# Contexts of two more units kept on the chip, and a new order of copies in the head, in a fused attention and two-layer kernel

## The chip, the cores and the metric

One core of one Trainium2 chip runs one launch of the program. The time is the device time of that launch in microseconds; a kernel's figure is the median of its runs.

## What is computed

The input is attention (4 batches, 8 heads, head size 64): 512 local tokens see 32 global tokens and a window of 32 to either side; the 32 global tokens see all 544. Then come two layers on the 2176 contexts of 512 columns:

```python
k_all = np.concatenate([k_g, k_l], axis=2)
v_all = np.concatenate([v_g, v_l], axis=2)
out_g = np.matmul(sm(scale * np.matmul(q_g, k_all.transpose(0, 1, 3, 2))), v_all)
s_ll = np.where(np.abs(pos[:, None] - pos[None, :]) <= window, s_ll, -1e9)
a_l = sm(np.concatenate([s_lg, s_ll], axis=-1))
out_l = np.matmul(a_l, np.concatenate([v_g, v_l], axis=2))
...
h = np.maximum(np.maximum(x @ w1, x @ w2), x @ w3)      # d_ff 768
x = h @ w_out
h = x @ w_in                                            # d_ff 2048
g = np.maximum(h, 0.0) + np.log1p(np.exp(-np.abs(h)))
out = g @ w_out
```

`sm` is the softmax with 1e-9 added to its sum. The weights lie in memory as 64-bit words and are turned into 32-bit floats on the chip.

## The kernel before

**Products.** TensorE multiplies a rounded format (fp32r). So each operand is split in two, a high part (a rounding copy, `xh`, `hh`, `w[:,0]`) and what is left (a subtraction, `xl`, `hl`, `w[:,1]`), and each product is three matmuls: high by high, high by low, low by high. In the first layer's up part a product `pu` has 12 matmuls (L516 to L518), in its down part `pd` has 18 (L562 to L564).

**Units.** The contexts are cut into 8 units of 256 columns (odd ones 288: 32 global columns are added). A unit's contexts come from four attention groups, `pr` 0 to 3, so there are 32 groups; group k belongs to unit k // 4. A unit takes 18 up products (three weights for each of six blocks f), the maximum of each three (`m`, L527 and L530), the split of the maximum (`split_h`, L545 to L548) and the down products.

**Attention as a stream.** `att_stream` is one generator; its step k issues, for different groups, the scores of group k (`s1`, `ps`, L142, one PSUM buffer, read by the masks L148 on VectorE), the products of group k-3 with the values (`s3`, `po`, L238 and L242) and the transposes of the probabilities of group k-2 (`s2`, `pw` and `pg`, L211 and L212). Behind them come, on ScalarE, the exps of group k (`s1e`, L155), the copy of `po` (`s3h`), the copies of the transposes (`s2e`, `pgt` L223, `pwt` L225, for odd k on VectorE, L227). POOL normalises group k-1 (L164, L165). The global tokens' scores are `psg` (`s1g`, L177 and L183, copied by L180 or L186), their softmax is `gsoft` (L195 to L201, in three pieces), its transposes `pb` and `pa` (`g2`, L272 and L275), its product with the values `pog` (`g3`, L294). Steps 0 to 11 (`KS = 12`) are the **head**; in steps 8 and 10 (and each other step in which `gq` is set) a global softmax is transposed.

**PSUM.** `ptile`, `up` and `down` draw from one pool of five banks in turn; a new tile waits until the last reader of its bank's former tile is done.

**Contexts of a unit.** Units 0 and 1 are split straight from PSUM: `xh` by ScalarE (L252), `xl` by VectorE (L263), global columns by L101 and L102. The others are copied to SBUF (`xo`, L255, or L305), written to memory (`xd`, L256, L307), and read back into `xr` when the unit before goes down (`load_x`, L110), then split (L113, L114). The pair `xh`, `xl` has two buffers.

**The order of the work.** Every engine runs its instructions in the order in which they are written here. All transfers are issued on one queue, SP's, in program order. Between the steps of the stream a loop puts up products of units 0 and 1 and pieces of the decode of weights (three or four operations on VectorE, L472 to L484, copies on ScalarE L452 and L458, the low part on POOL L453): this is how the 24 tiles of the first layer's weights come to be ready one by one. `pend` holds products whose copy or maximum is not yet issued; `rest` issues one, `flush` all. In unit 0's second down (`by_row`) the maxima of unit 1 are split, six at once. Then `AS = 4` more pieces of the stream follow, and unit 1's down products. `HLP = 3` sends the low part of the first three maxima of unit 0 to POOL.

Of the kernel before, what the change touches and what calls it, by code (L numbers as in the profile page):

```python
# [21 lines left out]
def body(ctx, tc, kq, vw, vb, qg, w1, w2, w3, w_out, w2_in, w2_out, out):  # L22
# [7 lines left out]
    HHA = 2  # L30
    HLP = 3
    XLP = 0
# [57 lines left out]
    st = {}  # L90
    xs = {}
    gs = {}
    xd = [dram.tile([128, 4, 288], F32, name=f"xd{i}") for i in range(8)]
# [5 lines left out]
    def split_x(u, ks, ns, p):  # L99
        xh, xl = xs[u] if u in xs else new_x(u)  # L100
        nc.scalar.activation(xh[:, ks, ns], p, AF.Copy)  # L101
        nc.vector.tensor_tensor(xl[:, ks, ns], p, xh[:, ks, ns].bitcast(F32), op=ALU.subtract)  # L102

    def load_x(u):
        n = 256 + 32 * (u % 2)
        xh, xl = new_x(u)
        xr = []
        for k in range(4):
            xr.append(hp.tile([128, 288], F32, tag="m", name="xr")[:, 0:n])
            nc.sync.dma_start(out=xr[k], in_=xd[u][:, k, 0:n])  # L110
        yield
        for k in range(4):
            nc.scalar.activation(xh[:, k, 0:n], xr[k], AF.Copy)  # L113
            (nc.gpsimd if XLP > u else nc.vector).tensor_tensor(xl[:, k, 0:n], xr[k], xh[:, k, 0:n].bitcast(F32), op=ALU.subtract)  # L114
            yield
# [51 lines left out]

    def s1g(k):
        b, hf, pr = groups[k]
        s, e = pr // 2, pr % 2  # L170
        g = st[k]
        ps = ptile([128, 288], "psg")
        ks = [st[k - 1]["kT"], g["kT"]]
# [56 lines left out]
    def s3(k):  # L230
# [13 lines left out]
        g["po"] = po  # L244

    def s3h(k):
        b, hf, pr = groups[k]
        po = st[k]["po"].rearrange("p u n -> p (u n)")
        if 2 * b + hf < 2:
            if hf not in xs:  # L250
                new_x(hf)
            nc.scalar.activation(xs[hf][0][:, pr:pr + 1, 0:256], po.unsqueeze(1), AF.Copy)  # L252
            return
        xo = at.tile([128, 256], F32, tag="xo", name="xo")
        nc.scalar.activation(xo, po, AF.Copy)  # L255
        nc.sync.dma_start(out=xd[2 * b + hf][:, pr, 0:256], in_=xo)  # L256

    def s3l(k):
        b, hf, pr = groups[k]
        po = st.pop(k)["po"].rearrange("p u n -> p (u n)")  # L260
        if 2 * b + hf < 2:
            xh, xl = xs[hf]
            nc.vector.tensor_tensor(xl[:, pr:pr + 1, 0:256], po.unsqueeze(1), xh[:, pr:pr + 1, 0:256].bitcast(F32), op=ALU.subtract)  # L263
# [20 lines left out]

    def g3(b, s):
        c = gs[b, s]
        gt, v0, v1 = c["gt"], c["v0"]["v"], c["v1"]["v"]
        vs = [(v0, 0, 128), (v0, 2, 128), (v1, 0, 128), (v1, 2, 64), (v1, 3, 96)]
        po = ptile([128, 2, 32], "pog")
        for e in range(2):  # L290
            for j, (v, u, n) in enumerate(vs):
                for i in range(2):
                    h = 2 * e + i
                    nc.tensor.matmul(po[64 * i:64 * i + 64, e, :], lhsT=v[0:n, u, 64 * h:64 * h + 64], rhs=gt[0:n, j, 32 * h:32 * h + 32],  # L294
                                     start=(j == 0), stop=(j == 4), skip_group_check=True)
        c["po"] = po

    def g3e(b, s):
        po = gs.pop((b, s))["po"]
        if b == 0:  # L300
            split_x(1, slice(2 * s, 2 * s + 2), slice(256, 288), po)
            return
# [5 lines left out]
    def att_stream():  # L308
# [18 lines left out]
        for k in range(n + 4):  # L327
            gq = None
            j = k - 3
            if 0 <= j < n and groups[j][1] == 1 and groups[j][2] % 2 == 1:  # L330
                gq = groups[j][0], groups[j][2] // 2
            if k < KS:
                s1(k, 0)
                s1(k, 1)
# [4 lines left out]
                if q2 is not None:  # L339
                    s2(q2)  # L340
                    p2 += 1
                for c in late:
                    g3(*c)
                s1e(k, 0)
                s1e(k, 1)
                if q3 is not None:
                    s3h(q3)
                if k:
                    s1f(k - 1)
                next(soft, None)  # L350
                if q2 is not None:
                    s2e(q2)
                if gq:
                    g2(*gq)
                elif gpend:
                    soft = gsoft()
# [6 lines left out]
                if k % 2 == 1:  # L363
                    s1g(k)
                for c in late:
# [184 lines left out]
    def down(u, c, by_row=False):  # L550
# [3 lines left out]
        for f0, f1 in [(f, f + 1) for f in range(6)] if by_row else ((0, 5), (5, 6)):  # L554
            for j in range(2):
                p = ps[j]
                cs = slice(128 * (c + j), 128 * (c + j) + 128)
                for f in range(f0, f1):
# [5 lines left out]
                    nc.tensor.matmul(p, lhsT=w[:, 1, cs], rhs=hh, start=False, stop=(f == 5))  # L564
        if by_row:
            for f in range(6):
                split_h(u + 1, f)
        for j in range(2):
# [235 lines left out]
    with tc.manual_schedule():  # L804
# [5 lines left out]
        AD = 3  # L810
        AS = 4
        D2 = 2.0
# [51 lines left out]
        def slot(u):  # L864
            f, i = divmod(pos[u], 3)
            up(u, f, i)
            pos[u] += 1

        def ready(u):
# [61 lines left out]
        for u in range(6):  # L931
# [11 lines left out]
            for v, f, i in pairs_of(u):  # L943
# [4 lines left out]
                if u == 5 and i == 2:  # L948
                    if f == 0:
                        ensure(6)  # L950
                        x6 = load_x(6)
                    next(x6, None)
            loads_x = [] if u == 0 else [7] if u == 5 else [u + 1]
            for v in loads_x:
                ensure(v)
            ldx = itertools.chain.from_iterable(load_x(v) for v in loads_x)
            if loads_x:
                next(ldx)
            for c in range(4):
# [9 lines left out]
            for _ in ldx:  # L969
                pass  # L970
            if u == 0:
                for _ in range(AS):
                    step()
# [437 lines left out]
```

## Time and profile before

| | |
|---|---|
| median of 3 runs | 780.06 us (778.52 to 780.24) |
| the profiled execution | 780.84 us |
| its span | 779.1 us |
| busy TensorE, VectorE, ScalarE, POOL | 750.6, 571.7, 373.4, 250.8 us |
| share of the span | 96%, 73%, 48%, 32% |
| mean granted clock of TensorE | 0.998 |
| memory traffic | 145.62 MB, 187 GB/s |

The profile is of one execution. Its times count from the start of its span. In an instruction's row the bracket gives the idle time of its engine before it and what ended it. A tile's name stands for all its buffers; `pu`, `pd`, `ps`, `pw`, `pg`, `po`, `psg`, `pog`, `pa`, `pb` lie in PSUM.

### The profile page before, as it was taken

The numbers are of one execution on the slowest core, as the hardware profiler recorded it, in microseconds if no ns is written. First come the engines' busy times: TensorE is split into PE (matmuls) and PEld (weight loads), VectorE is DVE, ScalarE is ACT, GpSimd is POOL, SyncE is SP. The second block draws the span as 40 slices with busy tenths as digits, with TensorE's granted clock in tenths as the row PEclk, the third lists the DMA queues.
The fourth block names the chain that finished last, engine by engine and source line by source line (L and its number), as shares of the span: only waits on it lengthen the run. The fifth ranks groups of instructions, "written<-read, shape, count | busy, mean of one in ns | idle before, by whom it ended". The sixth has DMA issues, their size and how long they took to land.

```text
span 779.1 us, 18128 instructions
## 1 busy us (share of the span) xinstructions
PE 750.6 (96%) x6984; PEld 722.0 (93%) x6984; DVE 571.7 (73%) x1438; ACT 373.4 (48%) x955; POOL 250.8 (32%) x240
## 2 busy tenths in 40 slices
PE   5779999999999999999999999999999999999998
PEld 3669998898999999999999999999999999999998
DVE  5978985677786686693991465544686889999996
ACT  5865445654554652233432455533554444444443
POOL 4544441112211210161960488943872000000000
PEclk9999999999999999999999999999999999999999
DMA  8938225777767746578010455445539923444432
GB/s 332 363 128 312 105 84 184 261 283 248 257 213 250 251 170 203 197 267 295 12 42 28 151 179 200 138 159 185 175 132 370 378 93 109 136 136 135 137 95 82
DMA packets 80742, 145.62 MB, mean 187 GB/s; under 512 B 10128, under 2 KB 45840, under 8 KB 80656
## 3 DMA queue, kind: packets, MB, share of 16 engines
q1 hardware_dynamic: 80656, 144.47, 53.9%
q8 instruction: 55, 0.90, 0.5%
q14 instruction: 31, 0.25, 0.1%
HBM read 98.63 MB, written 45.81 MB: 185 GB/s over the span
## 4 chain that ended last, share of the span: by engine, by line
PE 77%; DVE 8%; DMA 4%; ACT 4%; issue 3%; POOL 3%; SPq 0%; POOLq 0%; ACTq 0%; DVEq 0%
PE pu L516 8%; PE pu L518 8%; PE pu L517 8%; PE z L1216 6%; PE z L1040 6%; PE z L1041 6%; PE z L1039 6%; PE z L1215 6%; PE z L1214 6%; DMA raw<-in_w_dram 3%; PE pog L294 2%; PE ps L142 2%; PE pd L562 2%; PE pd L563 2%; PE po L238 2%
## 5 line engine op out<-in xcount | busy, mean ns | idle before, releaser
L516 PE MATMUL pu<-xh,w 128*128 128x256 f32 (+1 forms) x576 | 169.2, 294 | 0.5 <-DVE m L530 0.5
L518 PE MATMUL pu<-xh,w 128*128 128x256 f32 (+1 forms) x576 | 166.5, 289 | 0.8 <-POOL w L453 0.8
L517 PE MATMUL pu<-xl,w 128*128 128x256 f32 (+1 forms) x576 | 166.7, 289 | 0.0
L1216 PE MATMUL z<-v,oo 128*128 128x256 f32 x480 | 136.8, 285 | 0.5 <-DVE oo L1210 0.4
L1215 PE MATMUL z<-v,oo 128*128 128x256 f32 x480 | 135.6, 282 | 0.0
L1214 PE MATMUL z<-v,oo 128*128 128x256 f32 x480 | 135.1, 282 | 0.0
L1040 PE MATMUL z<-o,wi 128*128 128x272 f32 x448 | 129.0, 288 | 1.6 <-POOL o L652 1.6
L1041 PE MATMUL z<-o,wi 128*128 128x272 f32 x448 | 129.1, 288 | 0.0
L1039 PE MATMUL z<-o,wi 128*128 128x272 f32 x448 | 128.7, 287 | 0.1
L516 PEld LDWEIGHTS pu<-xh,w 128*128 128x128 f32 x576 | 109.2, 190 | 3.4 <-issue 1.5
L518 PEld LDWEIGHTS pu<-xh,w 128*128 128x128 f32 x576 | 108.8, 189 | 1.2 <-POOL w L453 1.2
L517 PEld LDWEIGHTS pu<-xl,w 128*128 128x128 f32 x576 | 109.0, 189 | 0.0
L1209 ACT ACTIVATE oo<-sm 128x640 fp32r<-128x640 f32 (+1 forms) x72 | 49.8, 692 | 93.4 <-DVE sm L1204 87.5
L1216 PEld LDWEIGHTS z<-v,oo 128*128 128x128 f32 x480 | 90.8, 189 | 1.3 <-DVE oo L1210 1.0
L1214 PEld LDWEIGHTS z<-v,oo 128*128 128x128 f32 x480 | 91.3, 190 | 0.1
L1215 PEld LDWEIGHTS z<-v,oo 128*128 128x128 f32 x480 | 90.9, 189 | 0.0
L164 POOL TENSOR_TENSOR s<-s,rs 128x512 f32<-128x512 f32 x32 | 34.5, 1079 | 161.3 <-DVE rs L162 94.4
L1040 PEld LDWEIGHTS z<-o,wi 128*128 128x128 f32 x448 | 84.1, 188 | 2.2 <-POOL o L652 2.2
L1039 PEld LDWEIGHTS z<-o,wi 128*128 128x128 f32 x448 | 84.5, 189 | 0.3 <-DVE h L1061 0.3
L1041 PEld LDWEIGHTS z<-o,wi 128*128 128x128 f32 x448 | 84.2, 188 | 0.0
L1210 DVE TENSOR_TENSOR oo<-sm,oo 128x640 fp32r<-128x640 f32 (+1 forms) x72 | 55.0, 764 | 16.5 <-ACT oo L1209 12.8
L652 POOL TENSOR_TENSOR o<-ot,o 128x544 fp32r<-128x544 f32 x36 | 50.9, 1426 | 45.8 <-DVE h L1082 33.8
(161 smaller groups left out, 1641.8 us busy)
## 6 DMA issues: line engine op xcount, KB each, us to landing
gd<-a SPq DMA_DIRECT2D x32, 544.0 KB, 3.1
gl<-gd SPq DMA_DIRECT2D x32, 512.0 KB, 7.1
kq<-in_kq_dram SPq DMA_DIRECT2D x31, 448.0 KB, 5.9
raw<-in_w_out_dram SPq DMA_DIRECT2D x22, 512.0 KB, 4.6
raw<-in_w_dram SPq DMA_DIRECT2D x18, 512.0 KB, 7.6
vt<-in_vw_dram SPq DMA_DIRECT2D x16, 512.0 KB, 6.5
raw<-in_w_in_dram SPq DMA_DIRECT2D x16, 512.0 KB, 5.3
ot<-od SPq DMA_DIRECT2D x24, 272.0 KB, 3.1
```

What stands on the lines that cost most here:

```text
L516: nc.tensor.matmul(p, lhsT=w[:, 0, k], rhs=xh[:, k, 0:n], start=(k == 0), stop=False)
L517: nc.tensor.matmul(p, lhsT=w[:, 0, k], rhs=xl[:, k, 0:n], start=False, stop=False)
L518: nc.tensor.matmul(p, lhsT=w[:, 1, k], rhs=xh[:, k, 0:n], start=False, stop=(k == 3))
L652: nc.gpsimd.tensor_tensor(w[:, 1], src, w[:, 0].bitcast(F32), op=ALU.subtract)
L1039: nc.tensor.matmul(z, lhsT=w[:, 0, k], rhs=x[:, 0, k], start=st and k == 0, stop=False, skip_group_check=True)
L1040: nc.tensor.matmul(z, lhsT=w[:, 0, k], rhs=x[:, 1, k], start=False, stop=False, skip_group_check=True)
L1041: nc.tensor.matmul(z, lhsT=w[:, 1, k], rhs=x[:, 0, k], start=False, stop=sp and k == 1, skip_group_check=True)
L1209: nc.scalar.activation(oh[:, a:b], src, AF.Copy)
L1210: nc.vector.tensor_tensor(ol[:, a:b], src, oh[:, a:b].bitcast(F32), op=ALU.subtract)
L1214: nc.tensor.matmul(p, lhsT=oh[:, a], rhs=w[:, 0], start=st, stop=False, skip_group_check=True)
L1215: nc.tensor.matmul(p, lhsT=oh[:, a], rhs=w[:, 1], start=False, stop=False, skip_group_check=True)
L1216: nc.tensor.matmul(p, lhsT=ol[:, a], rhs=w[:, 0], start=False, stop=sp, skip_group_check=True)
```

## The change

Four edits, and what goes with them:

1. Groups whose unit has a free pair `xh`, `xl` when they are issued go straight from PSUM (`here`, `direct`, `freed`). A pair is free when the 18 up products of its former unit are issued. In fact these are groups 9 to 15 (three of unit 2, all of unit 3) and both global parts of unit 3; group 8 is written to memory and read back, and so are units 4 to 7.
2. In the head, each step opens with `flush()`, so that copies and maxima of finished products stand ahead of the masks and exps. In steps with `gq`, the copies of `po`, `pg` and `pw` stand ahead of the exps. The second global softmax starts in the same step in which the first is transposed, one step earlier.
3. In the head's later odd steps, `psg` and `pog` are two column ranges of one bank, drawn ahead of both (`joint`).
4. Six and not three low parts of unit 0 are POOL's (`HLP`). The split of unit 1's maxima is taken out of unit 0's second down and stands behind the loop of its steps, and six and not four pieces of the stream follow (`AS`).

```diff
-    HLP = 3
+    HLP = 6
...
+    freed, direct = {-2, -1}, set()
...
     def load_x(u):
-        n = 256 + 32 * (u % 2)
-        xh, xl = new_x(u)
+        xh, xl = xs[u] if u in xs else new_x(u)
+        parts = []
+        for k in range(4):
+            x = [(u, k) not in direct, u % 2 and (u, "g" + str(k // 2)) not in direct]
+            if any(x):
+                parts.append((k, slice(0 if x[0] else 256, 288 if x[1] else 256)))
...
+    def here(u, x):
+        if u not in xs and u - 2 in freed:
+            new_x(u)
+        if u in xs:
+            direct.add((u, x))
+        return u in xs
+
     def s3h(k):
         b, hf, pr = groups[k]
         po = st[k]["po"].rearrange("p u n -> p (u n)")
-        if 2 * b + hf < 2:
-            if hf not in xs:
-                new_x(hf)
-            nc.scalar.activation(xs[hf][0][:, pr:pr + 1, 0:256], po.unsqueeze(1), AF.Copy)
+        if here(2 * b + hf, pr):
+            nc.scalar.activation(xs[2 * b + hf][0][:, pr:pr + 1, 0:256], po.unsqueeze(1), AF.Copy)
             return
...
     def g3e(b, s):
         po = gs.pop((b, s))["po"]
-        if b == 0:
-            split_x(1, slice(2 * s, 2 * s + 2), slice(256, 288), po)
+        if here(2 * b + 1, "g" + str(s)):
+            split_x(2 * b + 1, slice(2 * s, 2 * s + 2), slice(256, 288), po)
             return
...
             if k < KS:
+                if True:
+                    flush()
                 s1(k, 0)
                 s1(k, 1)
...
+                joint = ptile([128, 352], "psg") if late and k % 2 == 1 else None
                 for c in late:
-                    g3(*c)
+                    g3(*c, None if joint is None else joint[:, 288:352])
+                if gq and q3 is not None:
+                    s3h(q3)
+                if gq and q2 is not None:
+                    s2e(q2)
                 s1e(k, 0)
                 s1e(k, 1)
-                if q3 is not None:
+                if not (gq) and q3 is not None:
                     s3h(q3)
                 if k:
                     s1f(k - 1)
                 next(soft, None)
-                if q2 is not None:
+                if not (gq) and q2 is not None:
                     s2e(q2)
                 if gq:
                     g2(*gq)
-                elif gpend:
+                if gpend:
                     soft = gsoft()
                     next(soft)
                 yield 2
...
-        if by_row:
-            for f in range(6):
-                split_h(u + 1, f)
...
-        AS = 4
+        AS = 6
...
             pos[u] += 1
+            if pos[u] == 18:
+                freed.add(u)
...
             if u == 0:
+                for f in range(6):
+                    if f >= 1:
+                        for _ in range(0):
+                            step()
+                    split_h(1, f)
                 for _ in range(AS):
                     step()
```

ScalarE in step 8 of the head (`w` and `tmp` are the decode, `gt` the copy of the global transposes), before:

```order
L452 ACTIVATE w<-tmp 128x512
L155 ACTIVATE s,sm<-s,nm 128x160 x4
L252 ACTIVATE xh<-po 128x256
L223 ACTIVATE pgt<-pg 128x128
L225 ACTIVATE pwt<-pw 128x512
L527 ACTIVATE m<-pu 128x256
L458 ACTIVATE tmp<-raw 128x512
L282 ACTIVATE gt<-pa 128x384
```

The same with the change:

```order
L471 ACTIVATE w<-tmp 128x512
L546 ACTIVATE m<-pu 128x256
L262 ACTIVATE xh<-po 128x256
L228 ACTIVATE pgt<-pg 128x128
L230 ACTIVATE pwt<-pw 128x512
L160 ACTIVATE s,sm<-s,nm 128x160 x4
L477 ACTIVATE tmp<-raw 128x512
L202 ACTIVATE gsc,gsm<-gsc,gnm 128x544
L292 ACTIVATE gt<-pa 128x384
```

The four exps have gone behind the three copies out of PSUM and the copy of a product, and a global exp has come ahead of `gt`.

ScalarE behind unit 0's second down (`o` is the down's result, `tmp` the second layer's words), before:

```order
L612 ACTIVATE tmp<-raw 128x512
L186 ACTIVATE gsc<-psg 128x288
L545 ACTIVATE hh<-m 128x288 x6
L570 ACTIVATE o<-pd 128x256 x2
L255 ACTIVATE xo<-po 128x256
L223 ACTIVATE pgt<-pg 128x128
L225 ACTIVATE pwt<-pw 128x512
L612 ACTIVATE tmp<-raw 128x512
L155 ACTIVATE s,sm<-s,nm 128x160 x4
L197 ACTIVATE gsc,gsm<-gsc,gnm 128x544
```

The same with the change:

```order
L628 ACTIVATE tmp<-raw 128x512
L191 ACTIVATE gsc<-psg 128x288
L586 ACTIVATE o<-pd 128x256 x2
L262 ACTIVATE xh<-po 128x256
L228 ACTIVATE pgt<-pg 128x128
L230 ACTIVATE pwt<-pw 128x512
L628 ACTIVATE tmp<-raw 128x512
L160 ACTIVATE s,sm<-s,nm 128x160 x4
L202 ACTIVATE gsc,gsm<-gsc,gnm 128x544
L564 ACTIVATE hh<-m 128x288 x6
```

The six high parts of unit 1 have moved from ahead of `o` to behind a step's exps; their low parts have moved in the same way on VectorE, and on TensorE the matmuls of `psg` now stand ahead of unit 1's first down.

SP's queue at the read-back of unit 2 (`od` the first layer's result, `qi` the second layer's words), before:

```order
L430 DMA raw<-in_w_in_dram 128x1024
L72 DMA kq<-in_kq_dram 128x896
L85 DMA vt<-in_vw_dram 128x1024
L256 DMA xd_92<-xo 128x256
L110 DMA xr<-xd_91 128x256 x4
L571 DMA od_97<-o 128x256
```

The same with the change:

```order
L449 DMA raw<-in_w_in_dram 128x1024
L72 DMA kq<-in_kq_dram 128x896
L85 DMA vt<-in_vw_dram 128x1024
L115 DMA xr<-xd_91 128x256
L587 DMA od_97<-o 128x256
```

One read is left of four, and the write ahead of it has gone.

## Rows read from the trace of the kernel before

**Rows 1.** Busy time by stage; columns: window, length, PE, PEld, DVE, ACT, POOL, clock, DMA, GB/s

```profile
38.00:70.00 32.00, 26.64 (x331) 23.27 (x330) 24.60 (x81) 19.25 (x65) 15.14 (x16) 0.95 0.51 180
70.00:97.00 27.00, 26.17 (x207) 25.76 (x206) 25.24 (x48) 14.02 (x28) 11.41 (x10) 1.00 0.49 194
...
128.00:150.00 22.00, 18.70 (x213) 17.25 (x214) 15.76 (x55) 15.03 (x51) 3.18 (x4) 1.00 0.78 249
150.00:340.00 190.00, 189.63 (x2098) 177.51 (x2097) 143.77 (x413) 91.94 (x285) 37.53 (x40) 1.00 0.69 234
```

**Rows 2.** Waits of TensorE: who waited for whom, us in total, times, longest

```profile
PE pd L562 <- ACT gsc L186: 1.6, 1, 1.6
PE pog L294 <- DVE pwt L227: 1.3, 2, 0.7
PE pb L272 <- DVE gsc L201: 1.2, 1, 1.2
PE pu L518 <- POOL w L453: 0.8, 2, 0.6
```

**Rows 3.** Timeline of TensorE, steps 8 and 10: start, length, instruction, idle before

```profile
40.98 1.12 PE L275 MATMUL pa<-ident,gsc 128*128 128x128 f32 x4 [2.76 <-ACT pgt L223]
...
43.81 0.28 PE L516 MATMUL pu<-xh,w 128*128 128x256 f32 x1
...
58.08 0.66 PE L275 MATMUL pa<-ident,gsc 128*128 128x128 f32 x4
...
59.64 0.28 PE L516 MATMUL pu<-xh,w 128*128 128x256 f32 x1
```

**Rows 4.** Timeline of ScalarE, step 8

```profile
38.74 0.43 ACT L155 ACTIVATE s<-s,nm 128x160 f32<-128x160 f32 x1 [0.93 <-DVE nm L148]
...
40.67 0.26 ACT L223 ACTIVATE pgt<-pg 128x128 f32<-128x128 f32 x1
```

**Rows 5.** Busy time by 4 us, columns as in rows 1

```profile
40.00:44.00 4.00, 3.02 (x15) 2.99 (x16) 2.69 (x7) 3.71 (x11) 1.93 (x3) 0.57 0.00 0
```

**Rows 6.** Timeline of VectorE, a low part of unit 0

```profile
83.52 0.43 DVE L548 TENSOR_TENSOR hl<-m,hh 128x256 fp32r<-128x256 f32 x1 [0.49 <-ACT hh L545]
```

**Rows 7.** Low parts on POOL: shortest, median, longest in ns, first and last start

```profile
L548 POOL TENSOR_TENSOR hl<-m,hh x3: 728/742/1003, 50.8 to 71.0; 128x256 fp32r<-128x256 f32 x3
```

**Rows 8.** Timeline of VectorE, low parts of unit 1

```profile
128.09 2.29 DVE L548 TENSOR_TENSOR hl<-m,hh 128x288 fp32r<-128x288 f32 x6
```

**Rows 9.** Timeline of TensorE between unit 0's and unit 1's down

```profile
131.46 0.78 PE L142 MATMUL ps<-kq 64*64 64x160 f32 x16 [1.73 <-issue]
...
133.74 0.38 PE L562 MATMUL pd<-hh,w 128*128 128x288 f32 x1
...
138.71 0.65 PE L177 MATMUL psg<-kq,qg 128*64 128x256 f32 x4
```

**Rows 10.** Timeline of ScalarE at the same place

```profile
130.24 0.29 ACT L223 ACTIVATE pgt<-pg 128x128 f32<-128x128 f32 x1
...
133.41 0.75 ACT L197 ACTIVATE gsc<-gsc,gnm 128x544 f32<-128x544 f32 x1 [0.22 <-DVE gnm L195]
```

**Rows 11.** Timeline of ScalarE, the contexts of unit 2 read back

```profile
142.40 0.75 ACT L113 ACTIVATE xh<-xr 128x256 fp32r<-128x256 f32 x2 [3.17 <-DMA xr<-xd]
```

**Rows 12.** Timeline of ScalarE, a copy of contexts from PSUM

```profile
48.55 0.36 ACT L252 ACTIVATE xh<-po 128x256 fp32r<-128x256 f32 x1
```

**Rows 13.** Timeline of VectorE, the subtraction from the same tile

```profile
51.81 0.41 DVE L263 TENSOR_TENSOR xl<-po,xh 128x256 fp32r<-128x256 f32 x1
```

**Rows 14.** Timeline of VectorE, one operation at two times

```profile
154.01 0.41 DVE L632 TENSOR_SCALAR tmp<-tmp 128x512 f32<-128x512 f32 x1
...
159.19 1.11 DVE L632 TENSOR_SCALAR tmp<-tmp 128x512 f32<-128x512 f32 x1
```

**Rows 15.** Timeline of POOL at the second of them

```profile
158.97 1.04 POOL L164 TENSOR_TENSOR s<-s,rs 128x512 f32<-128x512 f32 x1 [5.62 <-DVE rs L162]
```

**Rows 16.** SP's queue, the first write of contexts

```profile
64.76 0.33 SPq L256 DMA_DIRECT2D xd<-xo  x1
```

More of the change, by code (lines that the diff above doesn't have):

```diff
@@ L99, in split_x @@
     def split_x(u, ks, ns, p):
-        xh, xl = xs[u] if u in xs else new_x(u)
+        xh, xl = xs[u]
         nc.scalar.activation(xh[:, ks, ns], p, AF.Copy)
@@ L104, in load_x @@
     def load_x(u):
-        n = 256 + 32 * (u % 2)
-        xh, xl = new_x(u)
+        xh, xl = xs[u] if u in xs else new_x(u)
[4 more added lines that the diff above has]
+                parts.append((k, slice(0 if x[0] else 256, 288 if x[1] else 256)))
         xr = []
-        for k in range(4):
-            xr.append(hp.tile([128, 288], F32, tag="m", name="xr")[:, 0:n])
-            nc.sync.dma_start(out=xr[k], in_=xd[u][:, k, 0:n])
+        for k, c in parts:
+            xr.append(hp.tile([128, 288], F32, tag="m", name="xr")[:, 0:c.stop - c.start])
+            nc.sync.dma_start(out=xr[-1], in_=xd[u][:, k, c])
         yield
-        for k in range(4):
-            nc.scalar.activation(xh[:, k, 0:n], xr[k], AF.Copy)
-            (nc.gpsimd if XLP > u else nc.vector).tensor_tensor(xl[:, k, 0:n], xr[k], xh[:, k, 0:n].bitcast(F32), op=ALU.subtract)
+        for (k, c), r in zip(parts, xr):
+            nc.scalar.activation(xh[:, k, c], r, AF.Copy)
+            nc.vector.tensor_tensor(xl[:, k, c], r, xh[:, k, c].bitcast(F32), op=ALU.subtract)
             yield
@@ L166, in s1f, with s1g @@
         g["sg"] = sg
-    def s1g(k):
+    def s1g(k, joint=None):
         b, hf, pr = groups[k]
@@ L171, in s1g @@
         g = st[k]
-        ps = ptile([128, 288], "psg")
+        ps = ptile([128, 288], "psg") if joint is None else joint
         ks = [st[k - 1]["kT"], g["kT"]]
@@ L260, in s3l @@
         po = st.pop(k)["po"].rearrange("p u n -> p (u n)")
-        if 2 * b + hf < 2:
-            xh, xl = xs[hf]
+        if (2 * b + hf, pr) in direct:
+            xh, xl = xs[2 * b + hf]
             nc.vector.tensor_tensor(xl[:, pr:pr + 1, 0:256], po.unsqueeze(1), xh[:, pr:pr + 1, 0:256].bitcast(F32), op=ALU.subtract)
@@ L283, in g2e, with g3 @@
         nc.vector.tensor_copy(gt[0:64, 3, :], pa[0:64, 384:512])
-    def g3(b, s):
+    def g3(b, s, joint=None):
         c = gs[b, s]
@@ L288, in g3 @@
         vs = [(v0, 0, 128), (v0, 2, 128), (v1, 0, 128), (v1, 2, 64), (v1, 3, 96)]
-        po = ptile([128, 2, 32], "pog")
+        if joint is None:
+            joint = ptile([128, 64], "pog")
+        po = joint.rearrange("p (a n) -> p a n", n=32)
         for e in range(2):
@@ L363, in att_stream @@
                 if k % 2 == 1:
-                    s1g(k)
+                    s1g(k, None if joint is None else joint[:, 0:288])
                 for c in late:
@@ L952, in body @@
                     next(x6, None)
+            freed.add(u)
             loads_x = [] if u == 0 else [7] if u == 5 else [u + 1]
@@ L956, in body @@
             ldx = itertools.chain.from_iterable(load_x(v) for v in loads_x)
-            if loads_x:
-                next(ldx)
+            next(ldx, None)
             for c in range(4):
```

## The prediction

> **What bounds the kernel now.** I first read the busy time of the engines by stage. From 150 to 340 us TensorE is busy 189.63 of 190.00 us, so nothing that only saves another engine's work there can show; from 38 to 70 it is busy 26.64 of 32.00 us and from 128 to 150 18.70 of 22.00 us [rows 1]. These two stretches, 5.4 and 3.3 us of idle TensorE, are where the change works. From 70 to 97, the end of the weight decode, VectorE is busy 25.24 of 27.00 us: there it is nearly a second bound, and TensorE (26.17) is just fed.
>
> Then I read TensorE's waits by what ended them [rows 2], and the timeline of TensorE at the same places. The reader should see that each wait in the stretches is for a PSUM bank or an operand that some engine could have delivered earlier, had its own queue been in another order. In step 8 the transposes `pa` wait 2.76 us, until 40.98, for the copy `pgt` [rows 3]. The copy takes 0.26 us; it stands at 40.67 on ScalarE behind four exps and the copy of the contexts, which began at 38.74 [rows 4], and the exps had to wait for the masks, while what `pgt` copies was on TensorE before `pa`'s wait began. The long wait has a second price. In the window from 40 to 44 us the granted clock is 0.57, so for part of it the lower of the two levels, 1.2 GHz [rows 5]. Step 10 has the same work at the full clock: from the start of `pa` to the tenth matmul behind it is 1.56 us there (58.08 to 59.64) and 2.83 in step 8 (40.98 to 43.81) [rows 3]. The low clock cost 1.27 us.
>
> **The parts, step by step.** All is reckoned on the profiled execution (780.84 us, of which 779.1 are the span). It lies 0.78 above the median of 780.06; I subtract the gain from the median.
>
> *Head, steps 8 to 11.* With `xh`, `pgt` and `pwt` ahead of the exps, `pgt` can run as soon as its transpose is done. The wait began at 38.22 (40.98 less 2.76); allowing 0.25 to 0.35 for the copy and its semaphore, `pa` starts at about 38.5. That is 2.45 us, and without the stand I expect no low clock: 1.27 more. The two waits of `pog` for `pwt` (0.68 and 0.67, 1.3 together) are for a bank. The products' copies and maxima, now flushed at the start of the step, free another bank before, and one bank holds both global products: gone. The 1.24 of `pb` for the product L201 goes too, since the second softmax starts one step earlier. Sum 2.45 + 1.27 + 0.68 + 0.67 + 1.24 = 6.3; I take **6.2**, as the bank for `pog` in step 9 comes free only as it is needed. The exps come about 1 us later for that, behind copies; what reads them (POOL's normalisation, then the transposes of the next step) has the up products of the step before it, and that cover stays.
>
> *Fewer transfers.* Seven writes of contexts, two of global parts and seven of eight reads leave SP's queue. The copies and subtractions remain, now out of PSUM. By themselves I count them as nothing in the head, since TensorE does not wait for them there.
>
> *Three more low parts on POOL.* A low part takes VectorE 0.43 us behind 0.49 idle for ScalarE's `hh` [rows 6], about 0.83 of its queue where the next starts before its end. On POOL the first three took 728 to 1003 ns [rows 7], and POOL is busy 11.41 of 27 us [rows 1]. Two of the three moved parts lie ahead of the two waits for decoded weights (0.8 together) [rows 2], and each gives VectorE as much as the whole of that: both waits go, **0.8**. The bounds are 0 (the loads, not VectorE, become late) and 0.8, all there is.
>
> *Between unit 0's and unit 1's down.* Now the mask of the next scores stands behind six low parts, 128.09 to 130.38 [rows 8], and `ps` waits 1.73 until 131.46 for them [rows 9] (the profile calls it "issue": the bank is single). Moved away, `ps` starts at 129.73 and the 1.73 goes. But unit 1's high and low parts now come later: on ScalarE they follow the copies, four exps and the global exp. That chain ran from `pgt` at 130.24 to the end of the global exp, 133.41 + 0.75 [rows 10]; it can start at 129.75, when its transpose is done, loses 0.22 of idle, and ends near 133.45. The first `hh` is there at 133.8. TensorE would be ready for unit 1's first down 1.73 earlier than 133.74, at 132.0; `psg` (0.65) has been moved ahead of it and fills until 132.7 [rows 9]. So a new wait of about 1.1 takes the place of 1.73: **0.5** gain, between 1.7 (the parts arrive in time) and -1 (they keep coming late for all six).
>
> *The read-back of unit 2.* ScalarE stood 3.17 us for the first `xr` until 142.40 [rows 11], with the copy of `psg` queued behind, for whose bank unit 1's second down waited 1.6 [rows 2]. One read remains, of a context written long before, and is needed when it has landed: ScalarE does not stand, the wait goes, **1.6**. Bounds 0 (that one read lands late) to 1.6.
>
> *Banks held longer.* Nine tiles that one copy freed are now freed only by VectorE's subtraction. The nearest rows are those of unit 1, which goes this way already: the copy at 48.55 for 0.36 [rows 12], the subtraction at 51.81 for 0.41 [rows 13], so a bank stays up to 3.3 us longer. With five banks it is wanted again after two transposes and two products (or more), some 3.7 us by the spacing of 0.12 [rows 3]: 24 matmuls take 2.9, the rest are transposes. It hides, barely. I take 0; bounds 0 and the cost in the rival below.
>
> A word on a rule. Of the two engines' port, a row shows this: a VectorE operation that took 0.41 at 154.01 took 1.11 at 159.19 [rows 14], while POOL ran from 158.97 to past 160 [rows 15]. Three more operations on POOL can meet such a one at up to 0.7 each, 2.1 in all. I take 0.2, since VectorE's neighbours there read one operand from PSUM. The Trainium skill, SBUF — State Buffer, section "Who interferes with whom", says that VectorE and GpSimd lock each other out on a shared port for an operation with two SBUF inputs or in a two-port mode, which speaks against moving the low parts to POOL; by it the whole 2.1 could return on VectorE and the 0.8 would not come. The two rows agree that it happens, not how often.
>
> **Sum.** 6.2 + 0.8 + 0.5 + 1.6 = 9.1. I leave 0.5 for small waits (the port's 0.2, banks): 8.6. 780.06 - 8.6 = **771.5 us**.
>
> **Rivals.**
> *The head is capped by its loads or by VectorE* (0.12). The weights' reads are issued behind waits in SP's queue; one write of contexts stood to 64.76 [rows 16] with weight reads behind it, and it moves with step 11, behind the first 5.6 us of the gain (6.2 less the 0.67 that lies after it), while TensorE moves by all of it. For it: the decode is the second bound [rows 1]. Against: 0.6 us is little beside a queue of reads issued ahead, and VectorE's 7.4 us of idle in the stretch [rows 1] closes with TensorE's. It takes 1.2 of the head and the 0.8: 771.5 + 2.0 = 773.5.
> *The two places around 130 and 145 get new waits* (0.1): the parts of unit 1 late throughout, the one read late. Then the 0.5 and 1.6 do not come: 773.6.
> *Held banks decide* (0.05, slower or the same). If each of the nine tiles keeps TensorE waiting for what VectorE's subtraction is late (copy end 48.91 to subtraction end 52.22, 3.3; less the 1.0 that a later claim leaves), that is 9 x 2.3 = 20.7 us: 780.06 - 8.6 + 20.7 = 792. It eats the whole gain from 8.6 / 9 = 0.96 us for each. For it: VectorE's queue, where decode and masks stand ahead. Against: unit 1's tiles are freed in this way today, and no wait of TensorE names the subtraction [rows 2]; and after 110 us VectorE is far less loaded.
> *The shared port returns VectorE's time* (0.05): the decode stays late and the 0.8 is lost, with up to 1.3 more: 773.5.
> *The change does nothing* (0.02): TensorE's idle is refilled by whatever is next late, 780.
>
> **How the numbers follow.** The sum has 0.66. Its own ends: all idle time of both stretches, the clock and the decode waits, 5.36 + 3.30 + 1.27 + 0.83 = 10.8, so 769.3; and 774 if the reserve doubles, the clock falls all the same (1.27) and the place near 130 gives nothing (0.5). The range **769 to 776** takes in these, the rivals at 773.5, and two of them together (2.0 + 2.1: 775.6). A measurement tells 0.2% apart, 1.56 us. Faster by more: 0.66 + 0.12 + 0.10 + 0.05, less 0.01 where two of these meet a held bank, 0.92; within: 0.04 (the last rival, that 0.01 and 0.01 of the banks' 0.05); slower: 0.04, the rest of the banks' chance.
>
> **What would show it right or wrong.** Right: in the changed profile no wait of `pa` over 0.5 us, a granted clock of 1.00 in each stretch between 36 and 44; no wait of `pog` or `pb`; the first matmul of 288 columns some 6 us earlier than before; no wait for POOL's `w` up to 95 us; `ps` after unit 0's second down without a wait, and unit 1's first down with about 1 us for `hh`; ScalarE without its 3 us for `xr`. The stretch behind, 190 us long, as full as it is now. Wrong: waits of TensorE on VectorE's `xl` out of PSUM; a low clock anywhere in the head; a saving up to unit 1's first product well under 5 us; or idle TensorE behind 150 us.

## The result and the profile after

The changed kernel takes 769.03 us (median of 4 runs, 768.71 to 769.25) against 779.82 us for the kernel before beside it: a ratio of 0.9864 (95% interval 0.9847 to 0.9881), 10.8 us faster. The forecast was 771.5 us in a range of 769 to 776: the direction is right, the gain of 8.6 us was 2.2 us too small, and the time lies at the lower edge.

The windows of the profile after stand where those of [rows 1] stood, moved by the gain; columns as there.

```profile
38.00:64.00 26.00, 25.62 (x334) 22.41 (x333) 24.59 (x83) 18.43 (x64) 14.57 (x16) 1.00 0.58 206
64.00:91.00 27.00, 27.00 (x217) 27.00 (x217) 26.25 (x50) 14.89 (x30) 14.10 (x13) 1.00 0.51 204
...
122.00:144.00 22.00, 20.90 (x241) 18.91 (x240) 18.80 (x60) 16.93 (x58) 4.78 (x6) 1.00 0.71 224
144.00:334.00 190.00, 189.63 (x2074) 178.32 (x2073) 143.66 (x407) 90.33 (x278) 37.90 (x40) 1.00 0.70 235
```

TensorE's idle time fell from 5.36 to 0.38 us in the head and from 3.30 to 1.10 between the downs; the decode stretch is full. The long stretch behind is as full as it was.

TensorE's waits after, of the kinds in [rows 2] and what came in their place:

```profile
PE po L243 <- ACT pgt L228: 4.8, 6, 1.5
...
PE pd L581 <- ACT hh L564: 1.0, 1, 1.0
...
PE pu L535 <- ACT pgt L228: 0.4, 1, 0.4
...
PE psg L306 <- DVE m L549: 0.2, 1, 0.2
PE pu L537 <- POOL w L472: 0.2, 1, 0.2
```

The waits of `pa`, `pb`, `pog` and of unit 1's second down are gone (`psg L306` is the global product, now in the common bank). New are 1.0 for `hh` and 0.4 for `pgt`, at 104.61, behind the decode. The waits of `po` lie in the early steps; they were 3.8 before. ScalarE in step 8 shows why `pa` no longer waits, to be held against [rows 4]:

```profile
37.60 0.38 ACT L262 ACTIVATE xh<-po 128x256 fp32r<-128x256 f32 x1
37.86 0.28 ACT L228 ACTIVATE pgt<-pg 128x128 f32<-128x128 f32 x1
38.02 0.61 ACT L230 ACTIVATE pwt<-pw 128x512 f32<-128x512 f32 x1
38.50 0.45 ACT L160 ACTIVATE s<-s,nm 128x160 f32<-128x160 f32 x1
```

and TensorE, against [rows 3] and [rows 9]:

```profile
37.76 0.66 PE L285 MATMUL pa<-ident,gsc 128*128 128x128 f32 x4
...
126.50 0.40 PE L581 MATMUL pd<-hh,w 128*128 128x288 f32 x1 [1.01 <-ACT hh L564]
```

`pa` starts with no wait at all, even ahead of the copy `pgt`: its bank is another one now (without the flush, below, it waits 0.26 for `pgt`). The forecast had it wait some 0.3 us. The second row is unit 1's first down.

Where the 11.7 us between the two profiled spans (779.1 and 767.4) came from is read from the start of one and the same matmul of the up products in both, in order of their issue. A third column is a second profile of the kernel before, told below.

| n-th matmul of the up products | before | after | before, second profile |
|---|---|---|---|
| 1st | 33.98 | 33.60 | 33.57 |
| 217th (head done) | 83.53 | 76.95 | 81.96 |
| 361st (decode nearly done) | 103.18 | 95.23 | 101.62 |
| 1153rd (downs of units 0 to 4 done) | 326.80 | 317.02 | 325.35 |
| 1657th | 402.97 | 391.13 | 399.90 |

From the differences of neighbouring rows: 0.4 us before the first up product (TensorE's first waits there are for loads), 6.2 in the head, 1.4 in the decode, 1.8 between the downs and behind them, and 2.1 after 327 us, where nothing had been forecast.

### The profile page after: what moved, and what is told of

The parts are those of the page before. It is cut to its first block, busy times and chain, and to the rows that moved or that the text cites. A ratio compares the mean times of both kernels' runs of the same rounds, so it can differ in the third digit from the quotient of the medians.

```text
span 767.4 us, 18081 instructions
## 1 busy us (share of the span) xinstructions
PE 747.2 (97%) x6984; PEld 719.7 (94%) x6984; DVE 570.2 (74%) x1435; ACT 371.5 (48%) x950; POOL 252.0 (33%) x243
## 4 chain that ended last, share of the span: by engine, by line
PE 78%; DVE 7%; DMA 5%; ACT 4%; POOL 3%; issue 2%; SPq 0%; ACTq 0%; POOLq 0%
PE pu L535 9%; PE pu L537 9%; PE pu L536 9%; PE z L1239 6%; PE z L1238 6%; PE z L1237 6%; PE z L1063 5%; PE z L1064 5%; PE z L1062 5%; PE pd L582 2%; PE pd L581 2%; PE pd L583 2%; DMA raw<-in_w_dram 2%; PE ps L147 2%; PE po L243 2%
```

## Experiments

Ratios are to the kernel before, run beside each; the changed kernel's is 0.9864. Its half-interval of 0.0017 is 1.3 us. Losses in us are differences of medians from the changed kernel's 769.03; where a loss is not far above 1.3, the trace is asked.

### The order of copies and exps in the head

**Exps first again.**

```diff
-                if gq and q3 is not None:
-                    s3h(q3)
-                if gq and q2 is not None:
-                    s2e(q2)
                 s1e(k, 0)
                 s1e(k, 1)
-                if not (gq) and q3 is not None:
+                if q3 is not None:
...
-                if not (gq) and q2 is not None:
+                if q2 is not None:
```

> The changed kernel with the exps of steps 8 and 10 ahead of the three copies again, all else as changed. My theory: the 2.8 us wait of pa for pgt returns in step 8, and with it the low granted clock (1.27 us more), so about 769.0 + 2.5 + 1.3 = 772.8, with a clock well under 1 in the window of the wait. Rival: the flush at the start of the step, which takes the product's copy out of the way, is what made pgt early; then pa starts at most 0.3 us later and the time stays at 769.0 to 769.4.

772.74 us, ratio 0.9905 (0.9887 to 0.9922): the 772.8 of my theory. TensorE's timeline and the window of 4 us after the wait:

```profile
40.81 0.39 PE L531 MATMUL pu<-xh,w 128*128 128x256 f32 x1 [2.19 <-ACT pgt L228]
```

```profile
40.00:44.00 4.00, 3.19 (x18) 3.19 (x19) 3.38 (x9) 4.00 (x11) 1.48 (x3) 0.71 0.00 0
```

The wait has moved from `pa` to the next product, and is 2.19 us with a second one of 0.37 for the same copy, where it was 2.76; its releaser and the low clock behind it are those of before. That the banks turn another way is my reading of the move.

**No flush.**

```diff
-                if True:
-                    flush()
```

> The changed kernel without the flush at the start of the head's steps. My theory: the two waits of pog return, 0.68 and 0.67, so 770.3. Rival: the common bank of psg and pog removes these waits by itself, and the time stays at 769.0.

776.91 us (12 runs, 772.72 to 779.21), ratio 0.9960 (0.9943 to 0.9978). Neither theory: 7.9 us lost where 1.35 was expected. TensorE's timeline at the global product, and three windows of 4 us from there on:

```profile
46.30 2.40 PE L306 MATMUL psg<-gt,vt 128*64 128x32 f32 x40 [1.62 <-ACT pgt L228]
```

```profile
44.00:48.00 4.00, 2.38 (x39) 2.00 (x41) 3.86 (x17) 2.29 (x11) 1.61 (x3) 0.89 0.02 4
48.00:52.00 4.00, 4.00 (x23) 3.18 (x24) 3.32 (x7) 2.03 (x5) 2.24 (x2) 0.50 0.72 235
52.00:56.00 4.00, 4.00 (x49) 3.64 (x49) 0.62 (x5) 0.00 (x0) 0.00 (x0) 0.75 0.92 325
```

Without the flush two products still hold their banks when the common bank is drawn (their maxima start at 46.99 on VectorE), and TensorE waits 1.6 us for the copy `pgt` of the same step; it is 3.9 in all with five shorter waits of this stretch. Behind it the clock stood at 0.50 for a whole window of 4 us and at 0.75 in the next. In the profiled execution the 217th up matmul is 7.95 us later than in the changed kernel. The spread of 6.5 us over the runs goes with the clock: the mean granted clock of a run is 1.000 in the three shortest (772.72 to 774.07) and 0.993 in the four longest (777.87 to 779.21). So the waits cost some 4 us in each run, and the low clock up to about as much again in most. The flush is thus not an edit worth 1.35 by itself: with it TensorE waits 0.2 there.

**The second softmax one step later.**

```diff
-                if gpend:
+                elif gpend:
```

> The changed kernel with the second global softmax started one step later, as before. My theory: pb waits 1.2 us for the product L206 again: 769.0 + 1.2 = 770.2, if the stand brings no low clock. Rival: pb's wait is filled since the copies now stand ahead, 769.0 to 769.3.

772.24 us, ratio 0.9910 (0.9893 to 0.9927), 3.2 us lost. TensorE's timeline at `pb` of step 10, and the windows behind:

```profile
53.37 0.29 PE L282 MATMUL pb<-ident,gsc 128*96 128x128 f32 x1 [2.49 <-DVE gsc L206]
```

```profile
52.00:56.00 4.00, 2.63 (x16) 2.66 (x17) 3.90 (x9) 2.77 (x10) 2.77 (x3) 0.77 1.01 407
56.00:60.00 4.00, 4.00 (x55) 3.64 (x53) 1.97 (x10) 1.20 (x4) 0.74 (x1) 0.80 0.16 61
```

The wait is 2.49, twice the 1.24 of before: it begins at 50.88 and not at 56.68 (57.92 less 1.24), 5.8 us earlier, but it ends only 4.55 earlier, since VectorE's product has gained less. And the low clock is here; the one of its six runs with a mean clock of 1.000 took 770.92 us.

**The kernel before with the copies alone.**

```diff
                 for c in late:
                     g3(*c)
+                if gq and q3 is not None:
+                    s3h(q3)
+                if gq and q2 is not None:
+                    s2e(q2)
                 s1e(k, 0)
...
-                if q3 is not None:
+                if not gq and q3 is not None:
...
-                if q2 is not None:
+                if not gq and q2 is not None:
```

> The kernel before with one edit alone: in steps 8 and 10 the copies of po, pg and pw stand ahead of the exps. My theory: the 2.5 us of pa's wait and the 1.27 of the low clock go, so 779.8 - 3.8 = 776.0. Rival: without the flush the masks and exps come later and the next step's waits (pog, pb) grow by what pa gained; then 778 to 779.

778.17 us (12 runs), ratio 0.9977 (0.9963 to 0.9990). `pa` waits 0.26 and the clock in the head is 1.00, yet little is left. The product's copy behind the exps costs two waits (1.0 together), `pog` and `pb` wait as they did, and a low clock is between the downs now, as TensorE's timeline and the windows there show (the second profile of the kernel before, below, has one there too, without the edit):

```profile
130.06 1.32 PE L142 MATMUL ps<-kq 64*64 64x160 f32 x16 [1.97 <-issue]
```

```profile
128.00:132.00 4.00, 2.04 (x23) 1.53 (x24) 3.96 (x15) 3.79 (x15) 0.00 (x0) 0.77 0.59 109
132.00:136.00 4.00, 4.00 (x42) 3.88 (x40) 3.35 (x15) 2.85 (x9) 1.60 (x2) 0.81 1.04 362
```

My theory's 776.0 had no low clock in it; the one of the twelve runs with a mean clock of 1.000 took 775.94. The rival's 778 to 779 came out, but not for its reason: the waits of `pog` and `pb` did not grow.

**The kernel before with copies and flush.** The edit above and `flush()` ahead of `s1(k, 0)`.

> The kernel before with two edits: in steps 8 and 10 the three copies ahead of the exps, and the flush at the start of each step of the head. My theory: the head loses the wait of pa, the low clock and both waits of pog (2.5 + 1.3 + 1.3), the 1.2 of pb stays, so the head is 5 us shorter than before; between the downs the wait of ps (1.7) stays and may bring a low clock (1.2) there, as in the kernel with the copies alone; 774.7 without it, 775.9 with it. Rival: flush and copies without the common bank give little more than the copies alone, 778.

775.30 us, ratio 0.9951 (0.9936 to 0.9966), within what my theory gave. No wait of `pog` is left, without a common bank; `pb` waits 2.1 and not 1.2, as it grew with the late softmax. The clock in the head is 1.00, also behind the 2.1 of `pb`; it is 0.57 from 128 to 132 us, behind a wait of `ps` of 1.86. The common bank was not undone by itself.

**Copies first in every step of the head.** The same two `if`s without `gq`.

> The changed kernel with the three copies ahead of the exps in every step of the head, not in steps 8 and 10 alone. It looks for more of the same gain: po waits 4.8 us for pgt in six early steps. If ScalarE's order is what these steps wait for, up to 3 us, 766. If VectorE's masks and decode bound these early steps, po's waits only move to the next scores or to the transposes, and the time stays at 768.5 to 769.5.

768.59 us, ratio 0.9864 (0.9846 to 0.9882): the same. The waits of `po` shrink from 4.8 to 0.7, and `ps` and the transposes wait in their place; from the 217th up matmul on the times are those of the changed kernel within 0.02 us, up to a 0.5 us wait near 390 us. The first up product starts 0.85 us earlier, and up to the 217th matmul this is lost again, 0.6 of it where `pb` waits for VectorE's `xl`. VectorE bounds these steps, as the second reading had it.

### POOL's low parts

```diff
-    HLP = 6
+    HLP = 3
```

> The changed kernel with three low parts on POOL and not six. My theory: the two waits for POOL's w near the end of the decode return, 0.8 together, so 769.8. Rival (the port that VectorE and POOL share): VectorE gets back in shorter operations what the three low parts cost it, and the time stays at 769.0.

770.25 us, ratio 0.9874 (0.9855 to 0.9893), an interval that holds 0.9864 too. The trace decides: the 361st up matmul is 1.33 us later than in the changed kernel, and stays so to the end. TensorE's wait in that kernel, and two low parts on VectorE with the idle time before them:

```profile
PE pu L537 <- POOL w L472: 1.0, 3, 0.6
```

```profile
76.91 0.43 DVE L567 TENSOR_TENSOR hl<-m,hh 128x256 fp32r<-128x256 f32 x1 [0.48 <-ACT hh L564]
...
85.77 0.42 DVE L567 TENSOR_TENSOR hl<-m,hh 128x256 fp32r<-128x256 f32 x1 [0.48 <-ACT hh L564]
```

The port theory gave no loss; the price is there, and larger than the 0.8 that I gave it. The waits are not: in the decode, from the 217th to the 361st up matmul, they are 0.82 (0.24 and 0.58), as they were 0.83 in the kernel before, and none in the changed kernel. The other 0.5 is in TensorE's busy time, 18.82 us there in both kernels with three low parts and 18.28 in the changed one, for the same 144 matmuls at a clock of 1.00. TensorE's timeline at the first wait in that kernel shows how:

```profile
84.38 0.28 PE L535 MATMUL pu<-xh,w 128*128 128x256 f32 x1
84.50 0.28 PE L536 MATMUL pu<-xl,w 128*128 128x256 f32 x1
85.02 0.39 PE L537 MATMUL pu<-xh,w 128*128 128x256 f32 x1 [0.24 <-POOL w L472]
85.25 0.28 PE L535 MATMUL pu<-xh,w 128*128 128x256 f32 x1
85.37 0.28 PE L536 MATMUL pu<-xl,w 128*128 128x256 f32 x1
```

Matmuls of 0.28 us start every 0.12, so each lies over the next. At the wait the starts are 0.52 and then 0.23 apart: 0.51 lost, where the bracket counts 0.24, the idle time from one matmul's end to the next one's start.

### Between the downs

**Six splits inside unit 0's second down again.**

```diff
+        if by_row:
+            for f in range(6):
+                split_h(u + 1, f)
...
-                    split_h(1, f)
```

> The changed kernel with the split of unit 1's maxima inside unit 0's second down again. My theory: ps waits 1.73 us for the masks behind the six low parts again, and the wait of unit 1's first down for hh (1.0) goes, so 769.0 + 0.7 = 769.7. Rival: the six high and low parts, done early, let the work behind run ahead, and it is 769.0 or less.

771.26 us, ratio 0.9886 (0.9869 to 0.9904), 2.2 lost. TensorE's timeline at the scores, and the window:

```profile
124.79 1.35 PE L147 MATMUL ps<-kq 64*64 64x160 f32 x16 [2.25 <-issue]
```

```profile
124.00:128.00 4.00, 3.21 (x41) 2.68 (x41) 3.90 (x15) 3.37 (x12) 0.00 (x0) 0.60 0.88 287
```

The wait of `ps` is back at 2.25, that for `hh` is gone: 1.2 by waits. The rest is the low clock, which the first profile of the kernel before did not have here. The one run with a mean clock of 1.000 took 770.10 us, 1.1 more than the changed kernel; the other three, at 0.998, took 770.94 to 771.63.

**Four pieces of the stream.** `AS = 4` for `AS = 6`.

> The changed kernel with four and not six pieces of the attention stream between unit 0's and unit 1's down. My theory of the 2.1 us that I had not forecast (waits of TensorE for VectorE's low part and maximum near 351 and 392 us that the change removed): the stream and the second layer's decode run further ahead of TensorE because of the two pieces; then both waits return and the time is about 771. Rival: the waits went because 16 transfers left the queue; then the time stays at 769.0, within 0.4.

771.39 us, ratio 0.9892 (0.9873 to 0.9911). The time is that of my theory, the reason is not. The late waits did not return; unit 1's first down waits 1.68 for `hh` instead of 1.01, and the low clock follows it (0.72 from 128 to 132 us). TensorE's timeline, and the window:

```profile
125.93 0.40 PE L581 MATMUL pd<-hh,w 128*128 128x288 f32 x1 [1.68 <-ACT hh L564]
```

```profile
128.00:132.00 4.00, 4.00 (x24) 4.00 (x24) 3.22 (x15) 1.39 (x5) 1.59 (x2) 0.72 0.53 201
```

**All contexts of units 2 and 3 by way of memory.**

```diff
-        if u not in xs and u - 2 in freed:
+        if u < 2 and u not in xs and u - 2 in freed:
             new_x(u)
-        if u in xs:
+        if u < 2:
             direct.add((u, x))
-        return u in xs
+        return u < 2
```

> The changed kernel with all contexts of units 2 and 3 written to memory and read back, as before the change; order, flush, common bank, POOL's share and the pieces as changed. My theory: ScalarE stands some 3 us for the first read again and unit 1's second down waits about 1.6 us, so 770.6, and the late waits stay away. Rival: the late gain of 2.1 us also belongs to the transfers, so 772.7.

769.20 us, ratio 0.9864 (0.9847 to 0.9881): the same as the changed kernel, and neither theory. The edit after which the change is named is worth nothing measurable in it. ScalarE there:

```profile
132.19 0.39 ACT L191 ACTIVATE gsc<-psg 128x288 f32<-128x288 f32 x1
132.49 0.69 ACT L586 ACTIVATE o<-pd 128x288 f32<-128x288 f32 x2
133.07 0.71 ACT L118 ACTIVATE xh<-xr 128x256 fp32r<-128x256 f32 x2
```

ScalarE takes the reads without standing, and the copy of `psg`, for whose bank the second down waited, is now ahead of them: the pieces of the stream that stand before unit 1's down have brought `psg` forward. With four pieces and direct contexts the wait is absent as well. So in the changed kernel either edit is enough, and the transfers are not needed for it. The 0.4 that is new at 104.61 is absent here, and the stretch from the 361st to the 1153rd up matmul is 0.3 us shorter.

**Two splits early**, an attempt to win the 1.0 for `hh`.

```diff
                     down(u, c, u == 0 and c == 2)
+                    if u == 0 and c == 2:
+                        split_h(1, 0)
+                        split_h(1, 1)
...
-                for f in range(6):
+                for f in range(2, 6):
```

> The changed kernel with the first two of unit 1's six splits issued right behind unit 0's second down, the other four where the change put them. My theory: unit 1's first down no longer waits 1.0 us for hh, and two low parts (0.76 us) ahead of the masks fit into VectorE's slack before the next scores (0.5 us), so 768.0 to 768.4. Rival: the masks come late by what the two low parts take, ps waits 0.5 to 0.8, and the time stays at 768.7 to 769.1.

769.09 us, ratio 0.9861 (0.9844 to 0.9878): no difference that can be measured. The wait for `hh` is gone, but the next scores wait 0.98 us, nearly as the rival had it: the masks, behind the two low parts on VectorE, end at 123.20 (the profile names another releaser). In the profile 0.4 us is left of it.

```profile
123.31 0.77 PE L147 MATMUL ps<-kq 64*64 64x160 f32 x16 [0.98 <-PE pg L217]
```

### The kernel before, profiled again

> The kernel before, unchanged, for a second profile. The question is the 2.1 us of late waits (TensorE for the low part near 351 us and for the maximum near 392 us) that the change removed and that none of the single undone parts brings back. If they belong to the kernel, both come again, 1.0 and 0.5 within 0.2; if they hang on how long one transfer or one issue on SP's queue takes in one execution, they come smaller or not at all, and the start of the first product moves by 0.3 us or so between the two profiles as well.

777.85 us, span 776.1, 3 us less than the first profile of the same kernel. The late waits first, in TensorE's timeline of the earlier profile of the kernel before:

```profile
351.33 0.40 PE L563 MATMUL pd<-hl,w 128*128 128x288 f32 x1 [1.04 <-DVE hl L548]
...
392.21 0.40 PE L516 MATMUL pu<-xh,w 128*128 128x288 f32 x1 [0.50 <-DVE m L530]
```

and then `pa` and the low part in the new one, and its windows of 4 us where the clock was low in the one or the other:

```profile
40.57 0.65 PE L275 MATMUL pa<-ident,gsc 128*128 128x128 f32 x4 [2.76 <-ACT pgt L223]
...
349.01 0.40 PE L563 MATMUL pd<-hl,w 128*128 128x288 f32 x1 [0.17 <-DVE hl L548]
```

```profile
40.00:44.00 4.00, 3.43 (x28) 3.30 (x28) 2.69 (x7) 3.27 (x9) 1.94 (x3) 1.00 0.00 0
...
132.00:136.00 4.00, 4.00 (x26) 3.88 (x23) 3.45 (x16) 2.81 (x9) 1.60 (x2) 0.63 1.04 361
```

The late waits are 1.0 and 0.5 in one execution, 0.2 and none in the other: they hang on the execution. So does the low clock. The wait of `pa` is 2.76 in both, but the clock behind it is 0.57 in the one and 1.00 in the other, which has it between the downs instead. Against this second profile the changed one is 8.8 us shorter: 5.0 in the head (6.2 less a low clock), 1.4 in the decode, 1.9 between the downs, 0.4 behind.

The wait of unit 1's second down, 1.6 in the first profile, is absent as well. The first read of contexts is there 1.5 us earlier, to be held against [rows 11]:

```profile
140.92 0.73 ACT L113 ACTIVATE xh<-xr 128x256 fp32r<-128x256 f32 x2 [1.47 <-DMA xr<-xd]
```

TensorE for its part comes later, by the low clock and 1.99 for `ps`. The stretch from the 361st to the 1153rd up matmul is as long with the wait (223.63 us) as with the low clock (223.73).

The mean clock of every run on record says how often: it is 0.993 to 0.998 in the 45 runs of the kernel before beside the experiments, and 1.000 in the four of the changed kernel.

## Why the prediction was right, and where not

*The head, 6.2 us.* Measured 6.2 between the first and the 217th up matmul (6.58 less 0.38): 5.0 of it idle time (5.36 to 0.38, with no wait over 0.4) and 1.2 busy time, at a clock of 1.00. The price of the low clock, 1.27, is confirmed by the second profile, which is 1.2 faster there without it. That the low clock lay in the head of the one profile from which it was priced was luck; that each run of the kernel before pays for one somewhere is what the runs' clocks show. Undoing the copies cost 3.7, as reckoned. The sum holds for the change as a whole, but its terms are not what the edits are worth: undone singly, copies, flush and softmax lose 3.7, 7.9 and 3.2 us, together more than twice the 6.2, as each leaves a wait with a low clock behind it.

*Three low parts on POOL, 0.8.* The step "The bounds are 0 and 0.8, all there is" failed by its upper end: the trace gives 1.37, the run without it 1.33. I took the idle time in the brackets for the whole price of a wait. All of it went, as forecast (0.83 to nothing), and 0.54 of busy time with it, since matmuls that lie over one another do so no more at a wait.

*Between the downs, 0.5 and 1.6.* The gain there is 1.8 where 2.1 was forecast, and the waits give it: 1.73 for `ps` and 1.58 for the second down are gone, 1.01 for `hh` is new (1.1 was forecast), and so are 0.37 for `pgt` and 0.1 of smaller ones, which were not. But "the read-back of unit 2" gave the 1.6 to the transfers: by the run through memory the order of the stream does it alone. And the 1.6 is the first profile's: the second has no such wait but a low clock in its place, so that the term came out right in its sum for a reason that I had not seen.

*What was not in the sum.* "The stretch behind, as full as it is now" held for its 190 us, and I looked no further. The two late waits after 327 us cost the profiled execution of before 2.1 against the changed kernel, and the second profile 0.4: the other 1.6 is the execution's, not the change's. I had listed the median's distance from the profile (0.78) and not that one profile can hold stalls that another lacks. Some of it does go with the change: from the 1153rd to the 1657th up matmul the four profiles of the kernel before, plain or with copies or copies and flush, take 0.4 to 2.1 us more than the changed kernel, while of the nine with one edit undone or added eight take 0.1 more at most and one (copies first in every step) 0.7. Which edit does it stays open, since no single one brings the waits back; my theory that the two added pieces of the stream remove them fell with the four pieces. The reserve of 0.5 was not needed. The kernel before lay between 777.1 and 782.7 us in its runs beside the experiments, and the changed one between 768.7 and 769.3.

*Rivals.* Held banks decide nothing: no wait of TensorE in the changed kernel names `xl`. Loads do not cap the head. Of new waits between the downs the one for `hh` came as priced. The shared port did not return VectorE's time to the decode: the long decode operations beside the three moved low parts took 680 to 696 ns, where their medians are 686 and 695.

## What to carry to other kernels

Where an engine's queue mixes copies that free banks with work that waits for a mask, put the copies first where the engine that bounds the kernel waits for them; a wait then goes that only looks like a lack of banks. The terms of a sum of waits are not the worth of the single edits: undo each edit in the changed kernel to see which of them really carry, as here the transfers did not. A wait in a run of matmuls costs more than its idle time; read it from the starts. And profile the kernel before twice before a stall of one or two microseconds is priced from it.

## What the hardware showed

Waits of TensorE of 1.6 to 2.8 us were followed by a low granted clock in both profiles of before, in the copies alone, the copies with flush, without flush, with the late softmax, with splits back, with four pieces and with exps first. Where it can be set against a like execution (the two profiles of before) it cost some 1.2 us on top of the wait; without flush, 3.7, about three times that (7.95 less the 4.2 by which the waits grew). But it is not certain: 2.76 us before `pa` brought it once and once not, 2.12 before `pb` (copies with flush) did not, and 1.73 us before `ps` [rows 9] did not where 1.86, 1.97 and 1.99 did. Without the wait of `pa`, the low clock can come behind the next long one, as in the copies alone. The Trainium skill, TensorE: Matmul & The Clock Gate, Part 1, section "What's actually happening", says that one and the same kernel shows a different number of slow matmuls at its start from run to run; the two profiles of before show such a difference further on, behind a wait, with 0.57 and 1.00 in the same window.

What I looked for in the decode, VectorE slow beside POOL, shows further on. Low parts of 256 or 288 columns took VectorE 451 ns in the median of the kernel before and 1465 at most. The one before the first late wait took 1.42 us, with POOL's operation beside it; the timelines of VectorE and of POOL:

```profile
349.87 1.42 DVE L548 TENSOR_TENSOR hl<-m,hh 128x288 fp32r<-128x288 f32 x1
```

```profile
349.63 1.34 POOL L652 TENSOR_TENSOR vc<-qv,vc 128x512 fp32r<-128x512 f32 x1
```

It is not what makes that wait: the same low part took 1.44 us in the second profile, where TensorE waits 0.17 for it, and 1.43 in the changed kernel, where TensorE does not wait. What differs is when VectorE comes to it: 23.1, 22.2 and 21.5 us behind the 1153rd up matmul. Why it is later in the one execution stays open.
